# Clearing a row block ahead of a group's transfers, and moving small steps of an attention schedule

## The chip, the cores and the metric

One core of a Trainium2 chip runs the whole program: bucketed attention, then a mixture of experts. The metric is the device time of one execution in microseconds. Three runs of the kernel before took 703.52, 703.8 and 705.65 us, median 703.8 us.

## The reference

There are 4 batches of 8 heads, 768 positions, head dimension 64. Each query and key gets a 6-bit hash (the signs of six projections). A query attends only to the keys of its own bucket, by a softmax. The rows of all heads are then put together to 3072 tokens of 512 numbers and sent, by a greedy assignment with a capacity of 384 tokens each, through 8 experts.

```
q_bits = (einsum('bhsd,dk->bhsk', q, proj) > 0)          # k_bits the same
mask   = q_bucket[:, :, :, None] == k_bucket[:, :, None, :]
scores = where(mask, scale * q @ k.T, -1e9)
attn   = softmax(scores); out = attn @ v                  # 32 heads
x      = out, heads side by side                          # 3072 x 512
order  = argsort(-(x @ w_gate)); each token to the best expert that has room
out[of e] = relu(x[of e] @ w1[e]) @ w2[e]
```

## The kernel before, in words

**Groups and operands.** The 32 heads are worked in 8 groups of 4 (`G` = 0 to 7). For a group, q and k come as 32-bit numbers (`load`, 768 KB each), are cast to 16 bits on ScalarE (`cast`, line 128: `qh`, `kh`), and what the cast drops is computed on GpSimd (`sub`, line 130: `ql`, `kl`). SyncE's DMA queue then brings the pieces into four operand tiles per group parity, `qa`, `ka`, `qb`, `kb` (`moves`, lines 174 to 185). The parity is `u = G%2`, so that group 2 overwrites the tiles of group 0, with tile numbers qa_180, ka_181, qb_182, kb_183 in the listings below; groups of odd number use 184 to 187.

**Rows of `qa`.** Rows 0 to 63 hold q. Rows 64 to 69 hold the hash signs, scaled by 8192 (`bits` on TensorE and VectorE, lines 142 and 143, `bscale` on ScalarE, line 144, then eight small DMAs, line 172, two per head). Rows 96 to 127 hold each query's maximum, in a form in which the product with `ka` subtracts it. Before a group's first pass those rows must be zero: `clear`, line 191, is one DMA that copies zeros (tile `wrm`) over the rows of all four heads, 192 KB. Groups 0 and 1 need none.

**Work of a head.** `S_pass` (line 240) computes 128 queries' scores against all keys in one pair of matmuls; it reads all 128 rows of `qa`, so it needs the cleared rows, the q rows and the signs of its head. VectorE takes the maximum (line 242). `m_rows` transposes the maxima (line 248) and ScalarE writes them into rows 96 to 127 (line 249). `ST` (lines 258, 259) computes the scores transposed, with the maximum taken off; ScalarE takes the exponential (line 260, tile `pt`). `lo` (line 263) computes what a 16-bit reading of `pt` drops, on GpSimd or, for the key blocks listed per head in `XL` (default `PAT`), on VectorE. `AV` (lines 273 to 275) multiplies by the values four steps later. At a head's end lines 279 and 280 add, out of rows 96 to 127 and a tile `wf`, the value sums of the group; `norm` (lines 287 to 290) divides and, every second head, sends two heads' rows to `x_dram` (line 293).

**Value sums.** `sumv` (lines 204, 206) sums a group's values on TensorE, 12 matmuls into one `pst` buffer that ScalarE copies out; `sumw` (lines 210 to 214) finishes `wf`.

**Order.** The program is written out engine by engine in the order in which Python emits it; nothing reorders it, and each engine's queue, SyncE's DMA queue too, runs strictly in that order. The loop over `t` (6 steps per head) has two half-steps 2t and 2t+1. A table `at` says which extra steps come at a half-step; `add(n,f,...)` puts one in. The tables at the file's head give the half-steps: `P1`, `P2`, `P3`, `P4` for the groups 1, 2, 3 and the later ones (in order: 8 casts, 4 subtractions, `bits`, two unused entries for the order of loads, start and steps of the value casts, `sumv`, loads), `MV` for `moves`, `CL` for `clear` (48(G-1)+CL), `BS` for `bscale` after `bits`, `SU` for group 0's `sumv`.

Two things follow for group 2: `moves` stands at half-step 59 and so did `clear` (48+11), behind it, since `add` appends:

```
if w==2: add(p[19+w],load,G,w)
...
if G>1: add(48*(G-1)+AP['CL'],clear,G)
```

In `moves`, group 2's order is q rows, the load of group 3's q, k rows, the low parts, signs, the load of group 3's k. The first pass of group 2, head 8, stands at about half-step 78.

Of the kernel before, what the change touches and what calls it, by code (L numbers as in the profile page):

```python
# [19 lines left out]
AP=dict(PAT=[[5], [3]],  # L20
 E0=[3, 5],
 E1=[3, 4],
 X=[2, 2, 5],
 MR=2,
 LEAD=9,
 S=[7, 7],
 DW=[12, 0, 0, 0, 384],
 P1=[13, 13, 14, 16, 17, 17, 23, 21, 16, 27, 21, 26, 23, 24, 33, 32, 3, 4, 49, -7, 3, 13],
 P2=[41, 44, 48, 49, 51, 51, 57, 55, 45, 49, 55, 57, 52, 60, 59, 61, 2, 3, 75, 32, 36, 47],
 P3=[69, 74, 83, 83, 85, 87, 88, 86, 77, 83, 87, 89, 94, 95, 96, 106, 0, 1, 120, 59, 63, 88],  # L30
 P4=[-33, -34, -25, -21, -13, -5, -9, -5, -18, -12, -3, 0, -5, 7, 10, 10, 3, 4, 36, -55, -50, -11],
 L0=[109, 2],
 EA=[[0, 0], [0, -1], [307, 4]],
 SW=4,
 XL={4: [0, 3, 5], 7: [1], 8: [0, 2, 4], 12: [2, 4, 5], 14: [0, 5], 18: [0, 5], 20: [0, 5], 29: [0, 1, 5], 30: [2]},
 BS=1,
 MV=[27, 59, 96, 1],
 CL=11,
 WS=-23,
 SU=16,  # L40
 OPS='b0 i3 i2 t0 w2 b1 w3 r0 r2 s0 w2 s1 C1 C0 r1 t1 c1 w4 s2 c0 w3 g0 l0 l1 u0 u1 B0 m0 a0 D0 s3 L0 L1 w2 e0 s4 d0 r3 l3 v2 v0 e1 w2 s5 e2 r5 l2 m1 s6 | s7 | x0 | s8 | v1 x1 | s9 | r4 s10 m2 | | s11 v3 f0 | x3 | | x2 m3 | | | | | |')
PAT,E0,E1,DW,LEAD=(AP[k] for k in ('PAT','E0','E1','DW','LEAD'))
NB=dict(S=2,T=3,V=1)
# [2 lines left out]
def attention(tc, nc, ctx, qT, kT, vv, proj, wg, x_dram, L, jp, identf, B, late=None, after=None):  # L46
# [84 lines left out]
    def bits(G,pairs):  # L131
        if (G,'b') not in TMP: TMP[G,'b']=dp.tile([128,S],F16,name="bt",bufs=1)
        bt=TMP[G,'b']; r=slice(0,128)
        ps=psS.tile([128,2,512],F32,name="pss")
        for hf in range(2):
            if G==0:
                for w in range(2):
                    T.matmul(ps[32*w:32*w+32,hf,0:384],pr,(qd,kd)[w][:,1,hf*384:hf*384+384],start=True,stop=True,tile_position=(0,32*w))
            for p in pairs:
                for w in range(2):  # L140
                    cg=64*p+32*w
                    T.matmul(ps[cg:cg+32,hf,0:384],pr,LD[G][w][:,p,hf*384:hf*384+384],start=True,stop=True,tile_position=(0,cg))
        V.tensor_scalar(bt.rearrange("p (z q) -> p z q",z=2),ps[:,:,0:384],0.0,0.5,op0=ALU.is_gt,op1=ALU.subtract)
# [51 lines left out]
    def sumv(G):  # L195
        u=G%2
        if G<2:
            A.copy(WF[u][96:128,:,64],wc[96:128,:].to_broadcast([32,4]))
        ps=psT.tile([128,512],F32,name="pst")
        n=0  # L200
        for c in range(6):
            for src in (VH[u],VL[u]):
                g=32*(n%4)
                T.matmul(ps[g:g+32,0:256].rearrange("p (j d) -> p j d",j=4),on,src[:,:,c,0:64],start=n<4,stop=n>7,skip_group_check=True,tile_position=(0,g)); n+=1
        SQ[G]=dp.tile([128,256],F32,name="sq",bufs=1)
        A.copy(SQ[G],ps[:,0:256])
# [54 lines left out]
    def lo(h,kc,eng):  # L261
        p,l=PT[h,kc]
        eng.tensor_tensor(l,p,p.bitcast(BF)[:,1::2],op=ALU.subtract)  # L263
# [18 lines left out]
    def norm(h):  # L282
# [8 lines left out]
        if hh%2:  # L291
            r=slice(64*hh-64,64*hh+64)
            SY.dma_start(x_dram[b*768:(b+1)*768,r].rearrange("(c p) d -> p c d",p=128),X[b][:,:,r])
    XH,XL=(XT[:,2*i:2*i+2].bitcast(F16).rearrange("p d c q -> p (d c q)").rearrange("p (d c q) -> p d c q",d=4,c=6) for i in range(2))
    def wsplit():
        A.copy(wgs[:,:,0],wgr); G_.tensor_tensor(wgs[:,:,1],wgr,wgs[:,:,0],op=ALU.subtract)
    def xtr(b,d,hf):
# [3 lines left out]
        A.copy(XH[:,d,r],p)  # L301
        V.tensor_tensor(XL[:,d,r],p,XH[:,d,r],op=ALU.subtract)
    LP=[]
    def logits(b,ds):
# [3 lines left out]
        for d in ds:  # L308
            for c in range(6): T.matmul(p[:,c],XH[:,d,c],wgs[:,d],start=(d==0 and c==0),stop=False,skip_group_check=True)
            for c in range(6): T.matmul(p[:,c,0],XL[:,d,c],wgs[:,d,0],start=False,stop=(d==3 and c==5),skip_group_check=True)  # L310
        if ds[-1]==3: V.reduce_sum(L[:,b*6:b*6+6],p.rearrange("p c z e -> p c e z"),axis=AX.X)
# [3 lines left out]
    def add(n,f,*a): at.setdefault(n,[]).append((f,a))  # L315
# [10 lines left out]
    for o in AP['OPS'].split():  # L326
# [2 lines left out]
        else: add(n,OPS[o[0]],int(o[1:]))  # L329
        if o[0]=='e': early.append(int(o[1:]))  # L330
    add(AP['WS'],wsplit); add(AP['SU'],sumv,0); add(AP['SU']+2,sumw,0)
    for G in range(1,NG):
        p=AP['P1'] if G==1 else AP['P2'] if G==2 else AP['P3'] if G==3 else [48*(G-1)+x for x in AP['P4']]
        st,sg=(AP['P4'] if G>3 else p)[16:18]
        for w in range(3):
            if w==2: add(p[19+w],load,G,w)
        for n in range(8): add(p[n],cast,G,n//2%2,n//4,n%2)
        for n in range(4): add(p[8+n],sub,G,n%2,n//2)
        add(p[12],bits,G,[0,1]); add(p[12]+AP['BS'],bscale,G); add(AP['MV'][G-1] if G<4 else 48*(G-1)+AP['MV'][3],moves,G)
        for j in range(4): add(p[15]+st*j,cv,G,j); add(p[15]+st*j+sg,sv,G,j,G_)  # L340
        add(p[18],sumv,G); add(p[18]+AP['SW'],sumw,G)
        if G>1: add(48*(G-1)+AP['CL'],clear,G)

    k=12; done={}; half={}; S_at={}
# [18 lines left out]
    def run(n):  # L363
        for f,a in at.get(n,[]): f(*a)
# [5 lines left out]
    for t in range(6*NH+LAG+6):  # L370
# [7 lines left out]
        if t>=1 and (t-1)//6<NH:  # L378
            hh,ss=divmod(t-1,6)
            lo(hh,ss,V if ss in (E0 if hh<1 else E1 if hh<2 else AP['XL'].get(hh,PAT[hh%2])) or t==6*NH else G_)  # L380
        run(2*t+1)
# [540 lines left out]
@with_exitstack  # L922
def tile_bucket_attention_moe(ctx, tc, qT, kT, vv, proj, wg, w1, w2, out):
    nc = tc.nc
    B = qT.shape[0] // 2
    drp = ctx.enter_context(tc.tile_pool(name="drp", bufs=1, space=DR))
    x_dram = drp.tile([768 * B, 512], F32, name="x_dram")
    M = Moe(tc, nc, ctx, 768 * B)
    late = M.consts()
    with ExitStack() as c1:  # L930
        c1.enter_context(tc.manual_schedule())
        attention(tc, nc, c1, qT, kT, vv, proj, wg, x_dram, M.Lm, M.jp, M.identf, B, late, M.early)
    with ExitStack() as c2:
        M.open(c2, x_dram, w1, w2, out)
        with tc.manual_schedule():
            M.start()
            M.run()
# [34 lines left out]
```

## Time and profile before

| what | value |
|---|---|
| median of 3 runs | 703.8 us (703.52 to 705.65) |
| profiled execution, its own time | 706.58 us |
| its span from first to last instruction | 704.4 us |
| TensorE matmuls busy | 664.3 us, 94% of the span |
| VectorE, ScalarE, GpSimd busy | 499.9, 472.1, 517.8 us |
| granted TensorE clock, mean | 0.972 of full |

The profiled execution's own time is 2.8 us above the median of the runs. Its span leaves 2.2 us of that time outside. Attention takes about the first half of the span, the experts the second; the change touches only attention. An engine's share over the whole span says little here: what a step costs is read from the stretch in which it stands.

### The profile page before, as it was taken

To read this page: it belongs to the slowest core of one execution; us is meant where nothing else is said; L and a number is where in the kernel's file an instruction comes from. 1 tells how busy PE (TensorE), PEld (TensorE's weight loads), DVE (VectorE), ACT (ScalarE), POOL (GpSimd) and SP (SyncE) were. 2 spreads that over 40 slices of the span, in tenths; PEclk is the share of its full clock that TensorE was granted. 3 is DMA by queue.
4 is the path that set the end of the run, shared out by engine and by line. 5 is a ranking of instruction groups with operands and counts; after the bars stand their busy time and mean duration, and the time that the engine had idled before them with its cause. 6 is when DMAs were issued, how large, how long until landed. Compare 5 with 4: busy or idle time off the path is not lost. (4 is left out here: it accounts for less than half of the span.)

```text
span 704.4 us, 19362 instructions
## 1 busy us (share of the span) xinstructions
PE 664.3 (94%) x7952; PEld 434.9 (62%) x7952; DVE 499.9 (71%) x1118; ACT 472.1 (67%) x886; POOL 517.8 (74%) x457
## 2 busy tenths in 40 slices
PE   8899979999999999999998589999999999999995
PEld 3566756776767767677766485555555555555552
DVE  6769848787977888878884678777787887834120
ACT  8878847787887878876764055756565656575840
POOL 7999978898898989988654256575766665677851
PEclk9999989999999999999999589999999999999998
DMA  9746842826537355350000171726262626363601
GB/s 225 206 116 183 193 139 52 211 71 139 145 100 189 95 140 154 98 118 24 24 25 26 49 237 21 282 76 251 88 242 86 244 82 233 98 247 104 227 29 45
DMA packets 39951, 93.58 MB, mean 133 GB/s; under 512 B 4548, under 2 KB 30520, under 8 KB 37816
## 3 DMA queue, kind: packets, MB, share of 16 engines
q1 hardware_dynamic: 33048, 46.21, 25.1%
q0 software_dynamic: 6816, 46.15, 18.5%
q8 instruction: 62, 1.02, 0.6%
q14 instruction: 25, 0.20, 0.1%
HBM read 59.53 MB, written 12.58 MB: 102 GB/s over the span
## 5 line engine op out<-in xcount | busy, mean ns | idle before, releaser
L263 POOL TENSOR_TENSOR lo<-pt 128x768 f16<-128x768 f32 x148 | 228.1, 1555 | 39.3 <-ACT pt L260 38.0
L260 ACT ACTIVATE pt<-pst 128x384 f32<-128x384 f32 x384 | 181.7, 491 | 64.1 <-PE pst L259 52.5
L242 DVE TENSOR_REDUCE m<-pss 128x1 f16<-128x770 f32 x192 | 181.1, 956 | 42.8 <-PE pss L240 42.1
L258 PE MATMUL pst<-qa,ka 128*128 128x384 f16 x384 | 125.7, 327 | 4.0 <-ACT qa L249 2.3
L259 PE MATMUL pst<-qb,kb 128*128 128x384 f16 x384 | 125.4, 327 | 0.0
L273 PE MATMUL psv<-vh,pt 128*128 128x65 f16 x1152 | 121.0, 195 | 1.1 <-DVE X L290 1.1
L274 PE MATMUL psv<-vl,pt 128*128 128x64 f16 x1152 | 121.1, 193 | 0.0
L275 PE MATMUL psv<-vh,lo 128*128 128x65 f16 x1152 | 121.1, 194 | 0.0
L273 PEld LDWEIGHTS <-pt 128*128 128x128 bf16 x1152 | 106.9, 98 | 9.1 <-issue 1.0
L274 PEld LDWEIGHTS <-pt 128*128 128x128 bf16 x1152 | 105.8, 99 | 9.5 <-issue 1.7
L275 PEld LDWEIGHTS <-lo 128*128 128x128 f16 x1152 | 106.0, 98 | 0.0
L240 PE MATMUL pss<-ka,qa 128*128 128x385 f16 x384 | 94.7, 330 | 6.4 <-issue 4.7
L782 POOL TENSOR_TENSOR wl<-wf,wh 128x512 f16<-128x512 f32 x72 | 82.7, 1172 | 21.7 <-ACT wf L773 21.2
L764 ACT ACTIVATE wh<-wf 128x1024 f16<-128x1024 f32 x64 | 67.0, 1051 | 35.6 <-PE psa L732 20.8
L842 PEld LDWEIGHTS <-wh 128*128 128x128 f16 x480 | 45.3, 97 | 30.0 <-issue 1.1
L854 PEld LDWEIGHTS <-hh 128*128 128x128 f16 x384 | 35.8, 97 | 38.6 <-issue 0.8
L773 ACT ACTIVATE wf<-wf 128x1024 f32<-128x1024 f32 x55 | 57.8, 1054 | 0.9
L240 PEld LDWEIGHTS <-qa 128*128 128x128 f16 x384 | 37.1, 97 | 32.4 <-issue 5.7
L263 DVE TENSOR_TENSOR lo<-pt 128x768 f16<-128x768 f32 x44 | 55.3, 1257 | 1.8 <-ACT pt L260 1.8
L857 ACT ACTIVATE o<-po 128x512 f32<-128x512 f32 x24 | 14.3, 595 | 62.5 <-PE po L854 51.9
L747 POOL DMA_INDIRECT xg<-x_dram,zidx x24 | 24.0, 1002 | 38.9 <-DVE zbnd L701 28.5
L755 POOL DMA_INDIRECT wf<-in_w_dram,zwidx x20 | 22.8, 1140 | 36.7 <-DVE zmi L688 20.6
(282 smaller groups left out, 1378.5 us busy)
## 6 DMA issues: line engine op xcount, KB each, us to landing
vp<-in_vv_dram SPq DMA_DIRECT2D x8, 768.0 KB
x_dram<-X SPq DMA_DIRECT2D x16, 384.0 KB
qp<-in_qT_dram SPq DMA_DIRECT2D x7, 768.0 KB
kp<-in_kT_dram SPq DMA_DIRECT2D x7, 768.0 KB
qa<-qh SPq DMA_DIRECT2D x14, 192.0 KB
qb<-qh SPq DMA_DIRECT2D x14, 192.0 KB
ka<-kh SPq DMA_DIRECT2D x14, 192.0 KB
kb<-kh SPq DMA_DIRECT2D x14, 192.0 KB
```

Of the source, the lines that this page charges most:

```text
L240: T.matmul(ps[:,hf,0:HK],QA[u][:,j,qc*128:qc*128+128],KA[u][:,j,hf*HK:hf*HK+HK],start=True,stop=True)
L242: V.tensor_reduce(M6[h][:,qc:qc+1],ps[:,:,0:HK],axis=AX.XY,op=ALU.max,negate=True)
L258: T.matmul(ps[:,0:384],KA[u][:,j,kr],QA[u][:,j,r],start=True,stop=False)
L259: T.matmul(ps[:,0:384],KB[u][:,j,kr],QB[u][:,j,r],start=False,stop=True)
L260: A.activation(PT[h,kc][0][:,r],ps[:,0:384],AF.Exp,scale=0.125)
L263: eng.tensor_tensor(l,p,p.bitcast(BF)[:,1::2],op=ALU.subtract)
L273: T.matmul(av[:,c,:],ph[:,r],VH[u][:,j,kc,:],start=(kc==0 and c==0),stop=False,skip_group_check=True)
L274: T.matmul(av[:,c,0:64],ph[:,r],VL[u][:,j,kc,:],start=False,stop=False,skip_group_check=True)
L275: T.matmul(av[:,c,:],l[:,r],VH[u][:,j,kc,:],start=False,stop=False,skip_group_check=True)
L764: s.nc.scalar.mul(h[:,r],f[:,r],WSC)
L773: s.nc.scalar.mul(f[:,r],f[:,r],WSC)
L782: for _ in range(n): s.nc.gpsimd.tensor_tensor(*s.pend.pop(0)[1],op=ALU.subtract)
```

## The change

**Row clearing.** `CL` goes from 11 to 9. For group 2 that puts `clear` at half-step 57, ahead of `moves` at 59. For groups 3 to 7 `clear` moves two half-steps earlier but stays behind the same DMAs.

**Value sums.** `sumv` of groups 1 to 6 no longer has a half-step of its own: it is emitted straight after the `bits` of the next group, and its `sumw` four half-steps later. Group 7 keeps its own; group 0's goes from half-step 16 to 15.

**Half-steps.** Group 1's second k cast goes from 16 to 15, its sixth cast (q, second pair, second half) from 17 to 21, its `moves` from 27 to 28; group 2's value casts start at 60 in place of 61; every `bscale` comes two half-steps after `bits` in place of one. (`P1`'s entry that goes from -7 to -6 is read by nothing.)

**Who computes `lo`.** Four more of the 192 low parts go to VectorE: key block 0 of heads 2, 6 and 10, and block 4 of head 7. Head 8 keeps three, at blocks 0, 3, 5 in place of 0, 2, 4.

```
- P1=[13, 13, 14, 16, 17, 17, 23, 21, ..., 49, -7, 3, 13],
- P2=[..., 59, 61, 2, 3, 75, 32, 36, 47],
+ P1=[13, 13, 14, 15, 17, 21, 23, 21, ..., 49, -6, 3, 13],
+ P2=[..., 59, 60, 2, 3, 75, 32, 36, 47],
...
- XL={4: [0, 3, 5], 7: [1], 8: [0, 2, 4], 12: ..., 30: [2]},
- BS=1,
- MV=[27, 59, 96, 1],
- CL=11,
+ XL={2: [0, 5], 4: [0, 3, 5], 6: [0, 5], 7: [1, 4], 8: [0, 3, 5], 10: [0, 5], 12: ..., 30: [2]},
+ BS=2,
+ MV=[28, 59, 96, 1],
+ CL=9,
...
- SU=16,
+ SU=15,
...
+    def hash_sum(G):
+        bits(G,[0,1])
+        if G>1: sumv(G-1)
...
-        add(p[12],bits,G,[0,1]); add(p[12]+AP['BS'],bscale,G); ...
+        add(p[12],hash_sum,G); add(p[12]+AP['BS'],bscale,G); ...
...
-        add(p[18],sumv,G); add(p[18]+AP['SW'],sumw,G)
+        if G==NG-1: add(p[18],sumv,G)
+        add((slots(G+1)[12] if G<NG-1 else p[18])+AP['SW'],sumw,G)
```

**Where it shows in the queues.** SyncE's queue around group 2's `moves`; before:

```order
L172 DMA qa_180<-bt 6x768
L172 DMA ka_181<-bt 6x768
L61 DMA kp<-in_kT_dram 128x1536
L191 DMA qa_180<-wrm 32x8x384
L293 DMA x_dram<-X 128x6x128
```

and with the change, at the head of the same transfers:

```order
L61 DMA vp<-in_vv_dram 128x1536
L293 DMA x_dram<-X 128x6x128
L191 DMA qa_180<-wrm 32x8x384
L174 DMA qa_180<-qh 64x2x768 x2
L176 DMA qb_182<-qh 64x2x768 x2
L61 DMA qp<-in_qT_dram 128x1536
L178 DMA ka_181<-kh 64x2x768 x2
L180 DMA kb_183<-kh 64x2x768 x2
```

The clearing (line 191) has moved from behind the last sign and the k load of group 3 to the place ahead of the first q row; it is the only row of SyncE's queue that moves.

TensorE's queue at group 2's hash bits (line 142, tiles qp and kp) with the change; the sums (line 204, values vh_223 and vl_224 of group 1) stand behind them, 12 pairs of rows of which two are shown:

```order
L142 MATMUL pss<-qp,pr 32x384
L142 MATMUL pss<-kp,pr 32x384
L204 LDWEIGHTS on
L204 MATMUL pst<-vh_223,on 32x256
L204 LDWEIGHTS on
L204 MATMUL pst<-vl_224,on 32x256
```

Before, those sums stood three half-steps ahead of these hash bits. Nothing is added to TensorE's queue and nothing taken out.

VectorE's queue in group 1, around head 5's end, with the change (m_1742 is the maximum tile of head 7, whose passes run while head 6 has its low parts made):

```order
L242 TENSOR_REDUCE m_1742<-pss 128x1 x2
L263 TENSOR_TENSOR lo<-pt 128x768
L242 TENSOR_REDUCE m_1742<-pss 128x1 x3
L263 TENSOR_TENSOR lo<-pt 128x768
L242 TENSOR_REDUCE m_1742<-pss 128x1
L287 TENSOR_SCALAR r_1962<-psv 128x6
L288 RECIPROCAL r_1962<-r_1962 128x6
L290 TENSOR_TENSOR X<-psv,r_1962 128x6x64
```

The second `lo` of this piece (head 6, block 0) is new here; before, four maxima of head 7 followed one another at this place.

## Rows read from the trace of the kernel before

**Rows 1.** The page: the span, and section 1, busy us of each engine.

```profile
span 704.4 us, 19362 instructions
PE 664.3 (94%) x7952; PEld 434.9 (62%) x7952; DVE 499.9 (71%) x1118; ACT 472.1 (67%) x886; POOL 517.8 (74%) x457
```

**Rows 2.** Waits of TensorE, whole span: waited for, us in total, times, longest.

```profile
PE pss L240 <- issue: 4.7, 1, 4.7
PE psv L273 <- DVE X L290: 1.1, 2, 0.6
```

**Rows 3.** Timeline of TensorE, 93.6 to 99 us: start, us, engine, instruction, [idle before].

```profile
93.71 0.33 PE L259 MATMUL pst<-qb,kb 128*128 128x384 f16 x1
98.79 0.48 PE L240 MATMUL pss<-ka,qa 128*128 128x385 f16 x1 [4.75 <-issue]
```

**Rows 4.** Timeline of SyncE's DMA queue, 0 to 135 us: start and length of an issue.

```profile
45.39 0.71 SPq L172 DMA_DIRECT2D ka<-bt  x1
...
73.31 0.38 SPq L293 DMA_DIRECT2D x_dram<-X  x1
74.21 1.31 SPq L174 DMA_DIRECT2D qa<-qh  x2
...
86.45 0.70 SPq L172 DMA_DIRECT2D ka<-bt  x1
...
91.87 0.38 SPq L61 DMA_DIRECT2D kp<-in_kT_dram  x1
92.36 0.72 SPq L191 DMA_DIRECT2D qa<-wrm  x1
94.76 0.39 SPq L293 DMA_DIRECT2D x_dram<-X  x1
```

**Rows 5.** Windows: stretch, length, busy us of engines, granted clock, DMA share, GB/s.

```profile
94.00:97.70 3.70, 0.04 (x1) 0.00 (x0) 0.70 (x2) 0.49 (x1) 3.70 (x3) 1.00 1.07 331
97.70:98.80 1.10, 0.01 (x1) 0.04 (x2) 0.00 (x0) 0.00 (x0) 0.26 (x1) 0.54 0.95 336
98.80:104.60 5.80, 5.80 (x34) 3.91 (x35) 2.98 (x4) 2.98 (x6) 1.50 (x2) 0.50 0.17 66
104.60:110.00 5.40, 5.40 (x87) 4.18 (x85) 4.03 (x4) 4.54 (x10) 3.67 (x3) 1.00 0.01 3
```

**Rows 6.** Windows of a later stretch, in which no clearing stalls anything.

```profile
160.00:200.00 40.00, 40.00 (x612) 28.80 (x612) 33.78 (x44) 34.69 (x80) 35.06 (x38) 1.00 0.58 146
```

**Rows 7.** Timeline of TensorE's weight loads, 90.2 to 90.8 us: group 2's sums.

```profile
90.28 0.23 PEld L204 LDWEIGHTS <-on 128*32 128x32 f16 x12 [0.32 <-issue]
90.73 0.10 PEld L273 LDWEIGHTS <-pt 128*128 128x128 bf16 x1 [0.22 <-issue]
```

**Rows 8.** Line 263, the low parts: duration in ns, least, median, most.

```profile
L263 POOL TENSOR_TENSOR lo<-pt x148: 1456/1466/2256, 22.3 to 378.0; 128x768 f16<-128x768 f32 x148
L263 DVE TENSOR_TENSOR lo<-pt x44: 945/962/2504, 25.9 to 379.2; 128x768 f16<-128x768 f32 x44
```

**Rows 9.** Timeline of VectorE, 84 to 124 us.

```profile
90.06 0.96 DVE L242 TENSOR_REDUCE m<-pss 128x1 f16<-128x770 f32 x1 [0.66 <-PE pss L240]
92.15 0.96 DVE L242 TENSOR_REDUCE m<-pss 128x1 f16<-128x770 f32 x1 [1.12 <-PE pss L240]
```

**Rows 10.** Timeline of GpSimd, 84 to 124 us.

```profile
89.22 5.73 POOL L263 TENSOR_TENSOR lo<-pt 128x768 f16<-128x768 f32 x4
...
101.27 1.47 POOL L263 TENSOR_TENSOR lo<-pt 128x768 f16<-128x768 f32 x1 [3.30 <-ACT pt L260]
```

**Rows 11.** Timeline of ScalarE: a copy of sums, group 3's first k casts.

```profile
91.11 0.36 ACT L206 COPY sq<-pst 128x256 f32<-128x256 f32 x1
...
106.77 0.92 ACT L128 CAST kh<-kp 128x384 f16<-128x384 f32 x2
```

**Rows 12.** Timeline of TensorE, 49.3 to 49.8 us: head 4's first pass, group 1.

```profile
49.51 0.49 PE L240 MATMUL pss<-ka,qa 128*128 128x385 f16 x2
```

**Rows 13.** Waits of TensorE, 30 to 40 us.

```profile
PE pst L258 <- ACT qa L249: 0.4, 1, 0.4
```

More of the change, by code (lines that the diff above doesn't have):

```diff
@@ L27 @@
  DW=[12, 0, 0, 0, 384],
- P1=[13, 13, 14, 16, 17, 17, 23, 21, 16, 27, 21, 26, 23, 24, 33, 32, 3, 4, 49, -7, 3, 13],
- P2=[41, 44, 48, 49, 51, 51, 57, 55, 45, 49, 55, 57, 52, 60, 59, 61, 2, 3, 75, 32, 36, 47],
+ P1=[13, 13, 14, 15, 17, 21, 23, 21, 16, 27, 21, 26, 23, 24, 33, 32, 3, 4, 49, -6, 3, 13],
+ P2=[41, 44, 48, 49, 51, 51, 57, 55, 45, 49, 55, 57, 52, 60, 59, 60, 2, 3, 75, 32, 36, 47],
  P3=[69, 74, 83, 83, 85, 87, 88, 86, 77, 83, 87, 89, 94, 95, 96, 106, 0, 1, 120, 59, 63, 88],
@@ L34 @@
  SW=4,
- XL={4: [0, 3, 5], 7: [1], 8: [0, 2, 4], 12: [2, 4, 5], 14: [0, 5], 18: [0, 5], 20: [0, 5], 29: [0, 1, 5], 30: [2]},
- BS=1,
- MV=[27, 59, 96, 1],
- CL=11,
+ XL={2: [0, 5], 4: [0, 3, 5], 6: [0, 5], 7: [1, 4], 8: [0, 3, 5], 10: [0, 5], 12: [2, 4, 5], 14: [0, 5], 18: [0, 5], 20: [0, 5], 29: [0, 1, 5], 30: [2]},
+ BS=2,
+ MV=[28, 59, 96, 1],
+ CL=9,
  WS=-23,
- SU=16,
+ SU=15,
  OPS='b0 i3 i2 t0 w2 b1 w3 r0 r2 s0 w2 s1 C1 C0 r1 t1 c1 w4 s2 c0 w3 g0 l0 l1 u0 u1 B0 m0 a0 D0 s3 L0 L1 w2 e0 s4 d0 r3 l3 v2 v0 e1 w2 s5 e2 r5 l2 m1 s6 | s7 | x0 | s8 | v1 x1 | s9 | r4 s10 m2 | | s11 v3 f0 | x3 | | x2 m3 | | | | | |')
@@ L331, in attention, with slots @@
     add(AP['WS'],wsplit); add(AP['SU'],sumv,0); add(AP['SU']+2,sumw,0)
+    def slots(G): return AP['P1'] if G==1 else AP['P2'] if G==2 else AP['P3'] if G==3 else [48*(G-1)+x for x in AP['P4']]
+    def hash_sum(G):
+        bits(G,[0,1])
+        if G>1: sumv(G-1)
     for G in range(1,NG):
-        p=AP['P1'] if G==1 else AP['P2'] if G==2 else AP['P3'] if G==3 else [48*(G-1)+x for x in AP['P4']]
+        p=slots(G)
         st,sg=(AP['P4'] if G>3 else p)[16:18]
@@ L338, in attention @@
         for n in range(4): add(p[8+n],sub,G,n%2,n//2)
-        add(p[12],bits,G,[0,1]); add(p[12]+AP['BS'],bscale,G); add(AP['MV'][G-1] if G<4 else 48*(G-1)+AP['MV'][3],moves,G)
+        add(p[12],hash_sum,G); add(p[12]+AP['BS'],bscale,G); add(AP['MV'][G-1] if G<4 else 48*(G-1)+AP['MV'][3],moves,G)
         for j in range(4): add(p[15]+st*j,cv,G,j); add(p[15]+st*j+sg,sv,G,j,G_)
-        add(p[18],sumv,G); add(p[18]+AP['SW'],sumw,G)
+        if G==NG-1: add(p[18],sumv,G)
+        add((slots(G+1)[12] if G<NG-1 else p[18])+AP['SW'],sumw,G)
         if G>1: add(48*(G-1)+AP['CL'],clear,G)
```

## The prediction

> **What bounds the kernel now.** I read the page first: TensorE is busy for 664.3 of 704.4 us and no other engine for over 74% [rows 1]. So only time in which TensorE stands still, or runs slowly, can be won; the change takes no matmul out. Next the waits of TensorE [rows 2]: the reader is to see that one single wait of 4.7 us is the longest of all, and that it carries no name, only "issue". The timeline puts it at 94.04 to 98.79 us, before the matmul of line 240 [rows 3], which by its place in the program is the first pass of head 8, group 2's first.
>
> What released it? Line 240 reads all rows of `qa`, so it needs the signs, the q rows and the cleared rows. The queue of SyncE [rows 4] shows the second sign of head 8 issued at 86.45 us, but the clearing only at 92.36, right behind a 768 KB load issued at 91.87. In 94.0 to 97.7 us the DMA engines are full (share 1.07, 331 GB/s), and still at 0.95 until 98.8 [rows 5]. The clearing's 192 KB had 768 KB ahead of them, about 2.4 us at 331 GB/s, and the store issued at 94.76 [rows 4] beside them. So I take it that line 240 waited for line 191. That is inferred from order and time; no row names it.
>
> The wait has a second price. The granted clock is 1.00 until 97.7, on average 0.54 in 97.7 to 98.8, 0.50 in 98.8 to 104.6 and 1.00 after that [rows 5]: after standing still, TensorE worked 5.8 us at the lower level, 1.2 GHz, and was busy all through. A later stretch of 40 us is busy for 40.00 at clock 1.00 [rows 6]: there nothing is to be won.
>
> **The change part by part.**
>
> *Clearing first.* One DMA issue of 0.72 us moves ahead of 22 others. It must wait until head 3's last read of `qa` is done, but the store of heads 2 and 3, issued at 73.31, stands ahead of it and waits for the same head's end; so it goes out at about 73.7, 20 us before it is needed. The q, k and sign transfers behind it are issued 0.72 us later: head 8's second sign at 87.2. How long such a sign takes to land no row shows; in group 1 the same sign was issued at 45.39 [rows 4] and head 4's first pass ran at 49.51 without a wait [rows 12], so 4.1 us is enough, and 91.3 is before 93.6, when TensorE now comes (next part). Wait left: 0. Its upper bound is the slowest landing near by, the clearing's own: 98.79 - 92.36 = 6.4 us, giving 93.6, no wait either. **Gain 4.75 us** [rows 3].
>
> *The clock.* Without the stop the 5.8 us at half clock become 2.9. **Gain 2.9 us.** The Trainium skill, "TensorE: Matmul & The Clock Gate", section Terms, prices throttled time as that time times the share of the clock lost. By that rule the 0.50 that began about 1 us before TensorE moved counts too, and the gain would be about 3.4; the row decides, since TensorE stood still in that first part anyway.
>
> *What limits the stretch then.* In 98.8 to 104.6 VectorE and ScalarE each had 2.98 us of work [rows 5], which now meets 2.9 us of matmuls. With the next stretch they have 2.98 + 4.03 = 7.0 and 2.98 + 4.54 = 7.5 us in 2.9 + 5.4 = 8.3. That is 84% and 91%; in the 40 us stretch they have 84% and 87% with TensorE never waiting [rows 6]. ScalarE is a little tighter: 4% of 8.3 us, **0.4 us given back** (bounds 0 and the whole 2.9).
>
> *The load behind it.* Group 3's k load now goes out 0.7 us later, at 92.6, and its first cast, at 106.77 before [rows 11], moves forward by 7.65, to 99.1. I take the load to have landed before 98.8 in the old order, as the clearing behind it had; in the new one before 99.5. ScalarE may wait 0 to 0.4 us; I take **0.3 given back**.
>
> *Sums behind the hash bits.* Six sums move by 3 to 19 half-steps, one by one. Each holds TensorE for 0.45 us (90.28 to 90.73 [rows 7]) at either place, so TensorE merely reaches head 8 at 93.6 in place of 94.04. Cost 0. Upper bound: each sum's copy on ScalarE, 0.36 us [rows 11], delays an exponential that TensorE needs: 6 x 0.36 = 2.2. Lower bound: nothing gained, since TensorE does not wait at the old places.
>
> *Four low parts from GpSimd to VectorE.* GpSimd is behind: four of them back to back at 89.22 to 94.95, and only the stop let it idle, 3.30 us before 101.27 [rows 10]. The change frees it of 2 x 1.47 us before that point (heads 2 and 6) [rows 8]. On VectorE each costs 0.96 to 2.50 us [rows 8]. Head 6's falls where VectorE idled 0.66 and 1.12 us [rows 9]; the other three lie in stretches with TensorE full. I take 0, bounds below. Here a rule speaks against the change. The rows show that a low part on VectorE takes 0.96 us at the median but up to 2.50, on GpSimd 1.47 but up to 2.26 [rows 8]: they do stretch each other. The Trainium skill, "SBUF — State Buffer", section Who interferes with whom, says that a VectorE instruction with two SBUF inputs and a GpSimd instruction that reads SBUF take turns, the loser blocked for the whole instruction. By it the relief for GpSimd is less than 1.47 us each, and the sum would lose what the second rival has.
>
> *Casts and `bscale`.* One q cast of 0.5 us leaves the place ahead of the maxima for which TensorE waited 0.4 us at 30 to 40 [rows 13]: **gain 0.3**. `bscale` one half-step later delays group 1's signs by about half a microsecond; the same 4.1 us cover it. `clear` in groups 3 to 7 keeps its place in the queue: 0. Group 2's value casts half a step earlier: 0.
>
> **Sum:** 4.75 + 2.9 + 0.3 - 0.4 - 0.3 = 7.25 us, taken as 7.2. Of the profiled execution's own 706.6 us that leaves 699.4. The median of the runs stands 2.8 us lower, at 703.8; I carry the same 7.2 over: **696.6 us**.
>
> **The rivals.**
>
> *Partial.* The stop goes, but the stretch that ran at half clock is held by ScalarE or VectorE, and the sums' copies cost something. For: their 2.98 us against 2.9 [rows 5], and waits of TensorE for VectorE's division, 1.1 us in two places [rows 2]. Against: they keep up at 84% and 87% later [rows 6]. Gain 4.75 - 0.3 - 0.9 (of the 2.2 for copies) = 3.5: 700.3 us.
>
> *Slower: VectorE and GpSimd block each other.* Place: heads 2, 6, 7 and 10. If each new low part on VectorE takes its longest, 2.50 us, delays the maxima behind it by that, and stretches a GpSimd one by 2.26 - 1.47 = 0.79, four cost 13.2 us if all of it reaches TensorE: 703.8 - 7.2 + 13.2 = 709.8. It decides against the change from 7.2 / 13.2 = 55% exposed. Against: VectorE's idle time before its maxima [rows 9]. The skill's port rule is this mechanism; the trace agrees that the two stretch each other, not that TensorE pays.
>
> *Not what it seems.* The nameless wait was for another transfer than the clearing, and stays. For: "issue" [rows 2]. Against: nothing else of group 2 was issued within a microsecond of it. Gain 0.3 - 0.3: 703.8.
>
> **How the numbers follow.** Forecast 0.73, partial 0.16, not what it seems 0.06, slower 0.05. A change of this kernel can be told from none by about 0.3%, 2.1 us. The forecast and the partial case are both faster: 0.89; same 0.06; slower 0.05. Lower end: full gains without anything given back, 4.75 + 2.9 + 0.4, and 0.6 of the waits on VectorE gone: 8.65, 695.1. Upper end: the partial case and its rounding, 700.5. The two together hold 0.89, less what falls past their ends.
>
> **What would show it.** Right: no wait of TensorE over 1 us before line 240 in the first 120 us; line 191 issued near 74 us; granted clock 1.00 all through 90 to 120; attention's later steps some 7 us earlier, and the experts' part as long as before. Wrong: a wait of several microseconds in the same place, now ended by a sign or a cast of `kh`; or waits for line 242 or 290 near heads 2, 6, 7, 10 that add up to more than 2 us.

## The result, and the profile after

The changed kernel took 696.55 us (median of six runs, 695.28 to 697.3), the kernel before beside it on the same chip 703.66 (702.01 to 706.63). The ratio is 0.9893, with a 95% interval of 0.987 to 0.9915: faster by 7.1 us, or 1.1%. Run again later (e5 below) it took 696.61, ratio 0.9884 (0.9862 to 0.9907).

The page of the kernel after, span and section 1, against [rows 1]: TensorE is busy for 4.3 us less with the same 7952 matmuls, and the span is 9.6 us shorter.

```profile
span 694.8 us, 19356 instructions
...
PE 660.0 (95%) x7952; PEld 435.0 (63%) x7952; DVE 502.0 (72%) x1122; ACT 472.2 (68%) x886; POOL 517.4 (74%) x453
```

The waits of TensorE after, whole span (waited for, us in total, times, longest), against [rows 2]:

```profile
PE pss L240 <- DVE m L242: 1.1, 1, 1.1
...
PE pst L210 <- ACT qa L249: 0.7, 1, 0.7
...
PE psv L273 <- DVE X L290: 0.5, 1, 0.5
```

The wait of 4.7 us without a name is gone, and of the two for line 290 one. Two are new: line 240 at 50.91 us (head 4's first pass; the row names a maximum, but e5 and e2 below show that it waited for a sign) and line 210, the second part of group 1's sums (at 74.71). SyncE's queue after, against [rows 4]:

```profile
74.03 0.71 SPq L191 DMA_DIRECT2D qa<-wrm  x1
...
88.60 0.70 SPq L172 DMA_DIRECT2D ka<-bt  x1
...
93.69 0.44 SPq L61 DMA_DIRECT2D kp<-in_kT_dram  x1
```

The clearing goes out at 74.03 and its last packet lands at 77.06 by the trace, long before head 8's first pass at 94.80 us. The signs went out 2.1 us later than before, at 88.60 in place of 86.45, and still head 8 did not wait. Windows after, for the stretches of [rows 5] (length; PE, PEld, DVE, ACT, POOL busy; granted clock; DMA share; GB/s):

```profile
94.00:97.70 3.70, 3.70 (x58) 2.66 (x55) 3.63 (x8) 2.59 (x6) 3.70 (x3) 1.00 0.75 239
97.70:98.80 1.10, 1.10 (x13) 0.82 (x10) 0.70 (x2) 0.70 (x2) 1.10 (x2) 1.00 1.07 286
98.80:104.60 5.80, 5.80 (x107) 4.54 (x105) 4.86 (x7) 5.65 (x13) 5.80 (x4) 1.00 0.40 140
104.60:110.00 5.40, 5.27 (x76) 3.16 (x76) 4.83 (x7) 3.86 (x9) 5.40 (x4) 1.00 0.17 36
```

Here the reader is to see that TensorE works through the place of the stop and that the clock stays at 1.00. GpSimd, which idled after the stop before [rows 10], is busy in all four stretches.

**Attention's own length.** The program has the same experts' part in all kernels, and yet from the last division of attention (line 288) to the end it took between 319.0 and 323.8 us in the 13 profiles. So besides run times I compare attention alone, from head 0's first wait of line 240 (at 10 to 11 us) to the last division. That last division stands at the second time of these rows, of the kernel before and of the kernel after (line 288, duration in ns, first and last start in us):

```profile
L288 DVE RECIPROCAL r<-r x32: 191/191/193, 35.3 to 381.7; 128x6 f32<-128x6 f32 x32
```

```profile
L288 DVE RECIPROCAL r<-r x32: 191/191/194, 36.9 to 374.1; 128x6 f32<-128x6 f32 x32
```

It came 7.6 us earlier. Attention alone took 371.3 us before and 363.5 after (363.7 when run again): 7.8 and 7.6 us less. The rest, 322.7 and 320.7 us, differs by no more than it does between the other profiles. The profiled execution of the kernel before took 706.58 us, 2.9 more than the median of its runs, so that what attention gained in a middling run isn't shown by it.

How much of attention TensorE was busy tells its work from its waits. Windows over attention, before and after (first numbers: stretch, length, TensorE busy):

```profile
10.45:381.73 371.28, 358.28 (x5519) 258.11 (x5519) 288.67 (x393) 287.69 (x612) 319.67 (x256) 0.99 0.46 120
```

```profile
10.65:374.10 363.45, 354.13 (x5519) 257.64 (x5519) 293.19 (x396) 287.32 (x612) 319.33 (x252) 1.00 0.47 123
```

The same 5519 matmuls took 4.15 us less, and the waits 3.68 us less, 9.32 in place of 13.00, though a single wait of 4.75 went.

### The profile page after: what moved, and what is told of

It is laid out like the page before. It is cut to its first block, busy times and chain, and to the rows that moved or that the text cites. A ratio compares the mean times of both kernels' runs of the same rounds, so it can differ in the third digit from the quotient of the medians.

```text
span 694.8 us, 19356 instructions
## 1 busy us (share of the span) xinstructions
PE 660.0 (95%) x7952; PEld 435.0 (63%) x7952; DVE 502.0 (72%) x1122; ACT 472.2 (68%) x886; POOL 517.4 (74%) x453
## 5 line engine op out<-in xcount | busy, mean ns | idle before, releaser
L263 DVE TENSOR_TENSOR lo<-pt 128x768 f16<-128x768 f32 x48 | 60.1, 1251 | 1.8 <-ACT pt L260 1.8
```

## The experiments

All times in us. "Attention" is one profiled execution, the length just defined.

| kernel | median of runs | ratio to before, 95% | attention |
|---|---|---|---|
| before (with e1 to e4; e5 to e8; e9 to e11) | 704.45; 704.08; 704.59 | 1 | 371.3 |
| e1 clearing early alone | 698.3 | 0.991 (0.9895 to 0.9925) | 364.7 |
| e2 the change, clearing late | 699.96 | 0.9944 (0.9924 to 0.9963) | 368.6 |
| e3 before, clearing ahead of the load | 699.8 | 0.9933 (0.9917 to 0.995) | 369.1 |
| e4 stop kept, clock kept | 702.98 | 0.9986 (0.9973 to 0.9998) | 369.0 |
| e5 the change again | 696.61 | 0.9884 (0.9862 to 0.9907) | 363.7 |
| e6 the change, sums as before | 699.78 | 0.9941 (0.9918 to 0.9965) | 367.0 |
| e7 the change, low parts as before | 696.47 | 0.9897 (0.9876 to 0.9917) | 364.0 |
| e8 the change, half-steps as before | 695.89 | 0.988 (0.9858 to 0.9902) | 364.3 |
| e9 sums one half-step behind the bits | 698.42 | 0.9908 (0.9885 to 0.9932) | 364.6 |
| e10 clearing and sums alone | 698.2 | 0.9903 (0.9879 to 0.9927) | 363.9 |
| e11 head 2 back, second part of sums later | 700.08 | 0.9931 (0.9908 to 0.9954) | 364.4 |

**e1: the clearing alone** (in the kernel before).

```
- CL=11,
+ CL=9,
```

> The kernel before with the clearing alone moved ahead of group 2's transfers. Theory (the nameless 4.75 us wait was for the clearing, and cost 2.9 us of clock besides): the wait and the half-clock stretch are gone; 4.75 + 2.9 less up to 0.7 given back, 696 to 697.5 us, as fast as the whole change or within 1 us of it, since the change's new waits of 1.1 and 0.7 us before 80 us are not there either. Rival (the low parts and the sums do a part of the work, since GpSimd is behind before the stop): waits for low parts or for VectorE appear at 95 to 115 us, and the time is 699 to 701. Rival (another transfer released it): 703 to 704.

Measured: 6.15 us off the median, 6.6 off attention; the median lies between the range of the theory and that of the first rival. The clock stayed at 1.00. So the clearing is most of the change, and some 1.2 us of attention are left for everything else. The waits that this kernel shares with the one before stand at 107.66 and 109.40 in TensorE's timeline; the changed kernel has neither:

```profile
107.66 0.19 PE L273 MATMUL psv<-vh,pt 128*128 128x65 f16 x1 [0.62 <-DVE X L290]
109.40 0.51 PE L142 MATMUL pss<-qp,pr 128*32 128x384 f32 x1 [0.38 <-DVE m L242]
```

**e2: all of the change but the clearing** (in the changed kernel).

```
- CL=9,
+ CL=11,
```

> The whole change with the clearing alone put back behind the k load. Theory: the wait before line 240 is back with 4 to 5 us and with it a stretch at clock 0.50 of about 7 us; 7 to 8 us slower than the change, 703.5 to 705 us, perhaps 1 us above the kernel before, because the change's own small new waits stay. Rival (other parts hold a part of the gain): 699 to 702.

**e3: the clearing between the last sign and the k load** (in the kernel before; for group 2, the other groups as they were).

```
- ... low(); signs(); nxt(1)
+ ... low(); signs(); clear(2); nxt(1)
- if G>1: add(48*(G-1)+AP['CL'],clear,G)
+ if G>2: add(48*(G-1)+AP['CL'],clear,G)
```

> The kernel before with the clearing one place further forward, between the last sign and the 768 KB load of group 3's k, so that it is issued half a microsecond earlier, at about 91.9 us. Theory that the clearing itself is only late because the load's bytes stand ahead of it: it lands about 2 to 3 us after its issue, near 94.5, TensorE waits 0.3 to 1.5 us, the clock stays at 1.00: 696.5 to 698.5 us. Rival that it was late because it was issued late: it gains the half microsecond and 703 us remain. Rival that line 240 waited for the load or a store: the wait stays at 4 us or more, 703 to 704.

TensorE's timeline of e2, then of e3, at head 8's first pass:

```profile
96.97 0.80 PE L240 MATMUL pss<-ka,qa 128*128 128x385 f16 x2 [2.73 <-DMA kp<-in_kT_dram]
```

```profile
96.74 0.50 PE L240 MATMUL pss<-ka,qa 128*128 128x385 f16 x2 [2.83 <-DMA qa<-wrm]
```

Both have the stop again, and e3 names the clearing as what ended it. In e2 the row names the k load, but by the trace that landed at 96.05; the clearing landed at 96.88, 0.1 us ahead of the pass. The stop was shorter than before, and neither theory was met: e2 came out in the range of its rival, e3 between its theory and its rivals. In e2 the clearing was issued 1.0 us earlier (91.32) and landed 5.56 us later, in place of 6.34. In e3, with no load ahead of it, it still took 4.42 us (92.27 to 96.69).

The trace tells the landing of the clearing in sixteen parts. Fifteen of them had landed 5.1 us after the issue in the kernel before (at 97.47), 5.5 in e2, and 2.9 in e3 (at 95.21): the load ahead was 2.2 to 2.6 us of the delay. The sixteenth part came 1.2 us behind the others before, 1.5 in e3 and 0.8 in e4. In all three the last 16 packets of the clearing began just as a packet of 16 KB ended (at 97.10, 94.84 and 97.44), of the queue that the page calls "instruction"; e2 had no such packet there, and its sixteenth part came 0.04 us behind the others. The page of the kernel before (packets, MB, share):

```profile
q8 instruction: 62, 1.02, 0.6%
```

So the stop before had three parts: the clearing went out late, 768 KB stood ahead of it, and one sixteenth of it landed 1.2 us after the rest. After both stops of e2 and e3 the clock was at half for 3.41 us by the trace's record, in place of 6.83 in the profile of before. Not every run seems to pay that: four of e2's six runs have a mean granted clock of 0.978 or 0.979 and took 699.3 to 700.4 us, the other two, the profiled one among them, 0.974 and 0.975 and 701.9 and 703.3. Windows of e2 (columns as above):

```profile
96.90:100.30 3.40, 3.33 (x14) 2.06 (x15) 1.21 (x2) 1.65 (x3) 1.74 (x2) 0.50 0.88 286
100.30:104.00 3.70, 3.70 (x55) 2.87 (x54) 2.76 (x5) 2.92 (x7) 2.09 (x2) 1.00 0.02 4
```

**e4: the stop kept, the clock kept** (in the kernel before; 18 matmuls on zeros, whose results nothing reads, ahead of head 8's first pass; they push line numbers by 3).

```
+ if (h,qc)==(8,0):
+     dps=psV.tile([128,512],F32,name="psv")
+     for _ in range(18): T.matmul(dps,wrm[:,0:128],wrm,start=True,stop=True)
```

> The kernel before with 18 matmuls on zeros (128 x 512 each, into a spare turn of the AV buffer) put ahead of head 8's first pass, so that TensorE works through most of the wait and the pass starts when the clearing lands, as before. It measures the price of the clock by itself. Theory: the pass still starts near 98.8 us, the granted clock stays at 1.00, and 2.9 us are won (bounds 2 and 3.4): about 700.8 us. Rival (VectorE and ScalarE, with 2.98 us of work each in that stretch, hold it): under 1 us won, 702.8 or more.

TensorE's timeline of e4, the zeros and the first pass, and the window that ran at half clock before [rows 5]:

```profile
95.27 4.06 PE L240 MATMUL psv<-wrm 128*128 128x512 f16 x18 [0.75 <-DVE X L293]
99.16 0.49 PE L243 MATMUL pss<-ka,qa 128*128 128x385 f16 x2
```

```profile
98.80:104.60 5.80, 5.52 (x63) 3.89 (x62) 3.86 (x6) 3.92 (x9) 2.94 (x2) 1.00 0.29 111
```

The first pass was held from 94.52 to 99.16, 4.64 us against 4.75. Attention is 2.3 us shorter, of which 0.1 is the shorter stop: the clock alone is worth **2.2 us** of attention. By TensorE's busy time it is 2.4 in e4, with the 3.9 us taken off in which only the zeros ran (95.27 to 99.16), and 2.6 in e1. Windows over attention, of e4 and of e1:

```profile
10.95:379.96 369.01, 359.76 (x5537) 258.26 (x5537) 288.56 (x393) 287.52 (x611) 319.85 (x256) 1.00 0.46 121
```

```profile
9.81:374.49 364.68, 355.73 (x5519) 256.44 (x5519) 288.15 (x393) 288.14 (x613) 319.63 (x256) 1.00 0.47 123
```

In the runs it is 0.0014 of the time, 1.0 us (0.1 to 1.9). The median, 702.98, is what the rival had, and not the 700.8 of the theory; but VectorE and ScalarE worked 3.86 and 3.92 us of those 5.80, so the rival's reason isn't seen. The mean granted clock was 0.973 in the 17 runs of the kernel before and 0.977 in e4's 12. That makes, by an estimate from these two, some 5 us less at half clock, where the profiled execution had 6.83; why the runs gained no more stays open.

**e5: the changed kernel again**, beside e6 to e8.

> The changed kernel itself, run again beside the three that undo one part of it, so that they share a chip. Expected: 696.5 us, ratio to the kernel before 0.9893 within 0.0015; the same waits of TensorE as in its first profile (line 240 for a maximum, 1.1 us near 51; line 210 for qa, 0.7 us near 75).

Measured: 696.61 us, and the same waits in the same places, but the one at head 4's first pass now has another name. TensorE's timeline of e5, then of e2, with VectorE's of e2:

```profile
50.75 0.49 PE L240 MATMUL pss<-ka,qa 128*128 128x385 f16 x2 [1.22 <-DMA qa<-bt]
```

```profile
50.18 0.49 PE L240 MATMUL pss<-ka,qa 128*128 128x385 f16 x2 [0.93 <-DMA ka<-bt]
```

```profile
49.39 0.95 DVE L242 TENSOR_REDUCE m<-pss 128x1 f16<-128x770 f32 x1
```

In e2 the pass began while the last maximum ahead of it was still being taken (49.39 to 50.34), so it can't have waited for that one. The pass writes one of two buffers (`psS`) and needs the maximum of two passes before; in the changed kernel that was done at 49.12. What it did wait for is the second sign of head 4: in the changed kernel this landed at 50.77 and the pass began at 50.91, in e5 at 50.61 and 50.75, in e2 at 50.04 and 50.18, and in e6 and e9 it is 0.14 us again.

**e6: the sums back at their own half-steps** (in the changed kernel).

```
- bits(G,[0,1])
- if G>1: sumv(G-1)
+ bits(G,[0,1])
...
- if G==NG-1: add(p[18],sumv,G)
- add((slots(G+1)[12] if G<NG-1 else p[18])+AP['SW'],sumw,G)
+ add(p[18],sumv,G); add(p[18]+AP['SW'],sumw,G)
```

> The changed kernel with the value sums of groups 1 to 6 back at half-steps of their own, where they stood before. Theory of the record (sums cost and win nothing): the time of the changed kernel, 696.5 within 0.7. Rival one (the sums behind the hash bits cost the 0.7 us wait of line 210 for qa that is new at 74.7, and the 0.4 and 0.25 behind it): that wait goes, and the time falls by 0.7 to 1.3, to 695.5. Rival two (the sums' move is what takes the 0.6 and 0.4 us waits of lines 273 and 142 away, which clearing early alone leaves at 107 to 110): those come back and the time rises by 1, to 697.5.

Measured: attention 3.3 us longer, the run 3.2. That is more than any theory gave. The waits at 107 to 111 came back (0.62 and 0.38, and 0.27 at 98), as rival two said. The wait of line 210 went, as rival one said, and 0.58 us of line 300 stand in its place. And two waits that no other kernel has came in, of line 248 for a maximum, 0.73 and 0.72 us, at 248.30 and 292.31. VectorE, GpSimd and TensorE of e6 around the first of them, and then VectorE and GpSimd of the kernel before at the same place of the program:

```profile
245.14 2.24 DVE L263 TENSOR_TENSOR lo<-pt 128x768 f16<-128x768 f32 x1
247.30 1.81 DVE L242 TENSOR_REDUCE m<-pss 128x1 f16<-128x770 f32 x2
```

```profile
245.09 1.47 POOL L263 TENSOR_TENSOR lo<-pt 128x768 f16<-128x768 f32 x1
```

```profile
248.30 0.23 PE L248 MATMUL pst<-ident,m 128*128 128x128 f16 x1 [0.73 <-DVE m L242]
```

```profile
250.90 0.95 DVE L263 TENSOR_TENSOR lo<-pt 128x768 f16<-128x768 f32 x1
```

```profile
251.52 1.66 POOL L263 TENSOR_TENSOR lo<-pt 128x768 f16<-128x768 f32 x1 [0.62 <-ACT pt L260]
```

In e6 GpSimd's low part began 0.05 us ahead of VectorE's; VectorE's then took 2.24 us in place of 0.95, the maxima behind it were late, and TensorE waited. Before, VectorE began first, took its 0.95, and GpSimd's took 1.66 in place of 1.47. The second wait has the same picture (GpSimd from 289.11, VectorE 2.23 us from 289.15). The Trainium skill, "SBUF — State Buffer", section Who interferes with whom, says that the order of issue decides which of the two blocks; the trace agrees, at 0.05 us. The two waits are 1.45 of the 3.3 us; how much of the rest is the sums' neighbourhood is what e9 was made for.

**e7: the low parts as before** (in the changed kernel).

```
- XL={2: [0, 5], 4: [0, 3, 5], 6: [0, 5], 7: [1, 4], 8: [0, 3, 5], 10: [0, 5], 12: ...
+ XL={4: [0, 3, 5], 7: [1], 8: [0, 2, 4], 12: ...
```

> The changed kernel with the list of low parts on VectorE as it was before (heads 2, 6, 10 and block 4 of head 7 back on GpSimd; head 8 at blocks 0, 2, 4). Theory of the record (worth nothing on the whole): 696.5 within 0.7, where the 1.1 us wait of line 240 for a maximum at 51 goes, and the 0.6 and 0.4 us waits of lines 273 and 142 come back near 107 to 110, one for the other. Rival (the relief of GpSimd matters beyond the waits that are seen): values wait for low parts on GpSimd again and the time rises by 1 to 2, to 698. Other rival (low parts on VectorE cost on the whole): 695.5.

Measured: 696.47 us, and attention 0.4 longer: as the record had it. Of the wait of line 240 at 51 0.2 us were left, and 0.3 and 0.4 us came at 106 to 108. Taking that wait away did not make attention shorter.

**e8: the half-steps as before** (in the changed kernel).

```
- P1=[13, 13, 14, 15, 17, 21, ...]   P2=[..., 60, 59, 60, ...]   BS=2   MV=[28, ...]   SU=15
+ P1=[13, 13, 14, 16, 17, 17, ...]   P2=[..., 60, 59, 61, ...]   BS=1   MV=[27, ...]   SU=16
```

> The changed kernel with the half-steps of group 1's casts and moves, group 2's value casts, bscale and group 0's sums back as they were before. Theory of the record (the casts win 0.3): 696.8, and the 0.4 us wait of line 258 for qa near 36 comes back. Rival (the moved steps win more than the wait that is seen, because signs and casts of ScalarE come at other places): 697.5 or more. Other rival (the new 0.2 us wait of line 248 at 35 makes up for it): 696.5.

Measured: 695.89 us, not to be told from the changed kernel. The 0.37 us wait of line 258 near 37 is back, and the 1.1 at 51 and the 0.7 at 75 are gone (0.6 of line 248 stands at 51 in its place); but its profile has a half-clock stretch of 3.41 us at 126 that e5's lacks, so the attention lengths can't be compared to the half microsecond. What the moved half-steps are worth is below what these runs can show.

**e9: the sums one half-step behind the bits** (in the changed kernel; a pair of matmuls, in one place a pass too, comes between).

```
- bits(G,[0,1])
- if G>1: sumv(G-1)
+ bits(G,[0,1])
...
- if G==NG-1: add(p[18],sumv,G)
+ add(slots(G+1)[12]+1 if G<NG-1 else p[18],sumv,G)
```

> The changed kernel, but the sums of groups 1 to 6 come one half-step after the next group's hash bits, with the pair of matmuls of lines 258 and 259 (in one place a pass of line 240 too) between. Theory now (what the sums win is the direct neighbourhood: from the start of the matmul ahead to the start of the one behind, bits and sum together take 0.21 us less where they touch than where other matmuls stand between): each of the six places takes 0.2 us more again, the hold of bits and of sum separately as in the kernel before (1.36 and 0.39 us between the end of the matmul ahead and the start of the next), 1.3 us in all, 697.8. Rival of the record (the sums' place is worth nothing): 696.5. Rival two (it is the half-step and the waits around it that count, not the touching): 696.5 too, with the same waits as the changed kernel has.

TensorE's timeline at group 4's bits, in e5 (the change) and in e9; the lines left out are the other bits and sums:

```profile
151.32 0.33 PE L258 MATMUL pst<-qa,ka 128*128 128x384 f16 x1
151.48 0.33 PE L259 MATMUL pst<-qb,kb 128*128 128x384 f16 x1
151.74 0.51 PE L142 MATMUL pss<-qp,pr 128*32 128x384 f32 x1
...
152.75 0.49 PE L142 MATMUL pss<-kp,pr 128*32 128x384 f32 x1
153.05 0.27 PE L204 MATMUL pst<-vh,on 128*32 128x256 f16 x1
...
153.50 0.34 PE L258 MATMUL pst<-qa,ka 128*128 128x384 f16 x1
```

```profile
152.63 0.49 PE L142 MATMUL pss<-kp,pr 128*32 128x384 f32 x1
153.05 0.34 PE L258 MATMUL pst<-qa,ka 128*128 128x384 f16 x1
153.23 0.33 PE L259 MATMUL pst<-qb,kb 128*128 128x384 f16 x1
153.39 0.49 PE L240 MATMUL pss<-ka,qa 128*128 128x385 f16 x2
153.81 0.28 PE L204 MATMUL pst<-vh,on 128*32 128x256 f16 x1
...
154.27 0.34 PE L258 MATMUL pst<-qa,ka 128*128 128x384 f16 x1
```

The column 128*32 or 128*128 is the part of the array that a matmul uses. From the last bit to the next matmul are 0.30 us where a sum follows, 0.42 where a 128*128 one does. From the last 128*128 matmul to the sum are 0.26 us (the second pass begins at 153.55) where such matmuls otherwise follow one another by 0.16 (151.32 to 151.48, the pair in e5). So a change from one use of the array to the other costs about 0.1 us each way; sums that touch the bits save one way out and one way in, 0.22 us, six times: **1.3 us**. The kernel before has the same: from the matmul ahead to the one behind are 1.69 us over bits and 0.71 over a sum wherever nothing is waited for, and 2.02 over both together in the changed kernel. That is 0.38 less, and with one ordinary step of 0.16 less to make, again 0.22. Attention in e9 is 0.95 longer than in e5, and from head 5's division to the end 1.1. The medians differ by 1.8, but their intervals overlap: the rows settle it, not the runs. The Trainium skill, "TensorEngine Tiling (Array Packing)", section Key Properties, says that changing the tiling mode drains TensorE; the trace agrees, at 0.1 us each.

**e10: clearing and sums alone** (in the kernel before: CL=9, and the new placement of the sums, as in the change).

```
- CL=11,
+ CL=9,
...
- add(p[12],bits,G,[0,1]); ...
+ add(p[12],hash_sum,G); ...
- add(p[18],sumv,G); add(p[18]+AP['SW'],sumw,G)
+ if G==NG-1: add(p[18],sumv,G)
+ add((slots(G+1)[12] if G<NG-1 else p[18])+AP['SW'],sumw,G)
```

> The kernel before with two edits alone: the clearing early and the sums of groups 1 to 6 straight behind the next group's hash bits; low parts, casts, moves and bscale as before. Theory now (these two are the whole change: 6 us for the clearing with its clock, 1.3 for the sums): 696.5, as the changed kernel. Rival (the low parts and the moved half-steps are needed for the rest): 697.5 to 698.5, near clearing alone, 698.3. Of the waits of TensorE, line 240 for a maximum near 51 should be gone and line 142 for a maximum near 107 back.

Measured: 698.2 us, in the range of the rival, while attention is the changed kernel's within 0.4 us. The wait of line 240 near 51 is gone, and that of line 142 didn't come back. Its timeline has a wait for an exponential that neither e1 nor the changed kernel has:

```profile
101.44 0.32 PE L258 MATMUL pst<-qa,ka 128*128 128x384 f16 x1 [1.11 <-ACT pt L260]
```

e7 and e8 each add one of the two parts that this kernel lacks, and neither has that wait. The divisions (line 288) say more than the sum: up to head 5's, e10 is 1.6 us shorter than the changed kernel, without the waits at 51 and 75 (82.9 and 84.5), and from there to head 11's 1.9 longer (69.9 and 68.0). So low parts and half-steps together lose early what they win later; whether they win in the run time is not settled.

**e11: a version that might have been better** (in the changed kernel: head 2 back on GpSimd, the second part of the sums two half-steps later).

```
- SW=4,
- XL={2: [0, 5], 4: ...
+ SW=6,
+ XL={4: ...
```

> A version that may be better than both: the changed kernel with head 2's block 0 back on GpSimd (it should take away the 1.1 us wait of line 240 near 51) and the second part of the sums six half-steps after the bits in place of four (it should take away the 0.7 us wait of line 210 near 75). If both waits go and nothing takes their place: 694.7. Rival (what TensorE does not wait for there it waits for at the next maximum or row of qa): 696 to 696.5.

Measured: 700.08 us. Both waits went, and others took their place (TensorE's timeline):

```profile
73.19 0.55 PE L300 MATMUL pst<-identf,X 128*128 128x128 f32 x3 [0.72 <-ACT qa L249]
...
106.59 0.19 PE L273 MATMUL psv<-vh,pt 128*128 128x65 f16 x1 [0.60 <-DVE X L290]
...
108.32 0.51 PE L142 MATMUL pss<-qp,pr 128*32 128x384 f32 x1 [0.38 <-DVE m L242]
```

Attention is 0.7 us longer than in e5. The other 2.7 us of its profile lie behind attention (323.8 against 321.1 us), where the two programs are the same and the clock was at half for 30.7 us in place of 27.3. Why, stays open. No version beat the changed kernel by what can be measured.

## Why the prediction was right, step by step

The forecast, 696.6 us, met the 696.55 measured; the two large terms hold, two of the small ones don't, and these cancel. Of the signs of being right one failed: a wait of 1.1 us stands before line 240 in the first 120 us, at 51.

- **What bounds the kernel, and the nameless wait.** Right. e3 names the clearing, e2 brings the stop back with all the rest of the change in place, e1 takes it away alone. The rival "not what it seems" falls. The 768 KB ahead of the clearing, put at 2.4 us, measure 2.2 to 2.6 in e3 against the two late clearings. What the argument didn't have is the sixteenth part of the clearing, 1.2 us of the stop.
- **Clearing first, 4.75.** Right: issued at 74.03 where 73.7 was forecast. The 0.72 us of issue came with 1.4 more, from transfers behind it that went out later, and the cover of 4.1 us for the signs was enough. TensorE came to head 8 at 94.80, not at 93.6: the new waits at 51 and 75 lie ahead of it.
- **The clock, 2.9, with 0.4 given back.** Right: 2.5 were forecast for the two, and TensorE's busy time in attention fell by 2.4 in e4 and by 2.6 in e1. Attention fell by less (2.2 in e4; e1's 6.6 leaves 1.9 beside the 4.75), since other waits grew by 0.3 and 0.7. (The 0.4 is a slip: 4% of 8.3 us are 0.33.) By the rule of the Trainium skill, "TensorE: Matmul & The Clock Gate", section Terms, it would be 3.4; the trace is below that. What limits the stretch is as expected: in 98.8 to 104.6 us ScalarE now works 5.65 of 5.80 us, and TensorE is busy in all 5.80.
- **The load behind it, 0.3 given back.** Mis-sized, it measured 0: the load landed at 98.34, and ScalarE reached its first cast at 99.75, without idling (its timeline; before, [rows 11]):

```profile
99.75 0.92 ACT L128 CAST kh<-kp 128x384 f16<-128x384 f32 x2
```

- **Sums behind the hash bits, 0.** This step failed. It took a sum to hold TensorE for 0.45 us "at either place". At the new place it and the bits together take 0.22 us less, for one change less between the two uses of the array each way: a gain of 1.3 in six places, partly used up by the new waits at 75 (0.72 of line 210, which goes when the half-steps are put back, in e8, and 0.38 behind it). The copies on ScalarE, the bound of 2.2, cost nothing that shows.
- **Low parts, 0 on the whole.** Right as a sum, from two parts that were not forecast. With the old list (e7) the stretch up to head 5's division is 0.5 to 0.8 us shorter, and from there to head 11's 1.4 longer. Head 2's low part took 2.15 us on VectorE, beside two subtractions on GpSimd that had begun before it, and so the last maxima of head 3 came late. VectorE and GpSimd of the changed kernel:

```profile
46.10 2.15 DVE L263 TENSOR_TENSOR lo<-pt 128x768 f16<-128x768 f32 x1
```

```profile
44.19 3.24 POOL L130 TENSOR_TENSOR kl<-kp,kh 128x768 f16<-128x768 f32 x2
```

  In e8 this costs 0.4 us (line 248 waits 0.59 us for a maximum at 51, 0.20 before). In the changed kernel it is hidden behind the longer wait of the next point. Outside the span lie 1.8 us in every run with the new list and 2.1 to 2.2 in every run with the old one; why, stays open.
- **Casts and `bscale`, 0.3.** The 0.4 us wait went, a 0.2 us wait of line 248 came at 35. The step on the signs failed: that "the same 4.1 us cover it". With the moved half-steps group 1's q rows go out straight ahead of its k rows (from 39.69 us on, in place of 35.86) and the signs behind both. Head 4's second sign was issued at 46.07 us in place of 45.39, took 4.7 us to land in place of 2.6, and the first pass waited:

```profile
50.91 0.49 PE L240 MATMUL pss<-ka,qa 128*128 128x385 f16 x2 [1.11 <-DVE m L242]
```

  The name in this row is that of the event that came last, not of the one that was waited for (e5). The wait needs head 2's low part too: with that back on GpSimd the sign took 2.7 to 2.8 us (e7, e11), with the half-steps back 2.5 (e8). How the low part comes to bear on the landing stays open. On the whole e8 finds nothing to measure.
- **The rivals.** "Partial" falls, since neither ScalarE nor VectorE held the stretch. "Slower" is a mechanism that exists: two places in e6 (0.73 and 0.72 us) show it whole, and e8 0.4 us of it at head 2. But it was priced at 3.3 us for each of four places, and in the changed kernel none of the four is shown to pay.

In all: 4.75 for the stop and about 2.5 for the clock, as forecast. The sums won 1.3 where nothing was forecast, and new waits took back 1.1 (the waits of attention fell by 3.7, not by 4.75) where none was; some 0.3 of the 7.8 is left without a place. Two errors of about a microsecond that cancel: that the number was met so closely is luck, and so is that a sum read from one profile, nearly 3 us above the median, held for the median.

## What to carry to other kernels

A wait without a name is read from the queue: look what was issued last of all that the waiting instruction reads, and whether it could go out before what stands ahead of it. Count a stop's price with the clock behind it, but from more than one profile, since the half-clock stretch was 6.8 us in one and 3.4 in others. A named releaser can be the event that merely came last: check it against the buffers, or against a second profile of the same kernel. When small matmuls move, look what part of the array their neighbours use, and put those that use the same part side by side.

## What was not expected of the hardware

- A change between 128*128 and 128*32 matmuls took about 0.1 us each way at full clock, with no wait shown for it.
- Which of two low parts is stretched turned on their order, in e6 by 0.05 us: 2.24 us for VectorE's when GpSimd's began first, 1.66 for GpSimd's when VectorE's began first.
- The same clearing of 192 KB took 3.0 us from issue to landing with little else under way (issued at 74.03). Fifteen of its sixteen parts took 2.9 us behind the signs and 5.1 to 5.5 behind a load; the sixteenth came 0.8 to 1.5 us later still where a 16 KB packet of the instruction queue ended just ahead of its packets.
